# One core, an attention and a mixer: the load order of k and v, with all schedule tables redone

## The chip, the cores and the metric

One core of a Trainium2 chip. The metric is the device time of one execution in microseconds, median of several runs; lower is better. The profile is one execution taken by the hardware profiler. Engines: PE is TensorE (PEld its weight loads), DVE is VectorE, ACT is ScalarE, POOL is GpSimd, SP is SyncE, which only issues DMAs here.

## What is computed

Four batches (b = 0 to 3) of a linear attention with decay, and behind each a mixer over tokens and channels. All inputs and the output are float32.

```
B, H, S, D = 4, 8, 768, 48
for t in range(S):
    cur = einsum('bhd,bhe->bhde', u * k[t], v[t])
    y[t] = einsum('bhd,bhde->bhe', r[t], state + cur)
    state = w * state + einsum('bhd,bhe->bhde', k[t], v[t])
x = y as (B, S, 384)
h = relu(x^T @ w_tok1) @ w_tok2         # tokens: 768 -> 256 -> 768
u = x + h^T
out = u + relu(u @ w_ch1) @ w_ch2       # channels: 384 -> 1536 -> 384
```

## The kernel before, in words

**Attention.** A batch's 768 steps are six chunks of 128 (c = 0 to 5). Below, k2.3 is the load of k for batch 2, chunk 3, and so on. A load of k, v or r of one chunk is 192 KB in rows of 192 bytes (tiles kt, vt, rt, six, six and five buffers); for batches 0 and 1, r comes in windows of two chunks (tile win, 384 KB, r0.0, r0.2, r0.4). For each chunk k and r are multiplied by tables of decay (tile kr), turned, multiplied with each other to scores (at_ps), masked (AT), and multiplied with v (vb, its bfloat16 copy) to y_ps, to which the state's part is added. A state (kv_ps, S) goes from chunk to chunk. The own term (u times k times r, then times v) is summed over each head (adg) and multiplied with vb (tile ydb or yd); that last product is called own2.3 here. In batches 0 and 1 the turning is done on TensorE (tk, tr_all, result evacuated to rka and rkb), the own sum as a product (pr) and matmuls (sm); in batches 2 and 3 by DMA transposes from SP's queue (T2.3; tile rk) and with products on GpSimd (ku, rku, and two for kr: about four per chunk and own). x_b is a chunk's result. The scores of batches 2 and 3 are formed for two chunks at once (sc2.0 means chunks 0 and 1 of batch 2).

**Mixer.** Per batch: hidden (h1), back projections with the sum u (hT_ps, hx_ps; turned into uT on TensorE, or by DMA, U2.0), 24 up projections (z_ps, relu to zr) and 18 groups of down projections of 4 matmuls (h_ps), sums to osb and stores (st2.3). Weights come as seven DMAs from GpSimd's queue with conversion to bfloat16: w0 and w1 (the two token matrices, tile wtok), w2 and w3 (first third and rest of the first channel matrix), w4, w5, w6 (thirds of the second; all four kinds in tile wch). An up projection of the first four of twelve column blocks needs w2, the others w3; a down part j needs w4 + j.

**Order.** Nothing decides at run time. Some 900 tasks are added in a fixed numbering (a `Plan`); `ORDER` lists the task numbers in the order in which they are emitted, and every engine and every DMA queue works through its own tasks in that order. `BUFS` gives the buffer that each use of a tile takes, `ENGINES` picks one of the two engines for tasks that can run on either. SP's queue holds all loads, DMA transposes and nearly all stores; a load waits there until its buffer is free, and all behind it wait with it. Two tables tie the queues together:

```python
def load_weights(i):
    def f():
        t, src, how = parts[i]
        sent[i] = pool.dma_start(t, src.rearrange(how, p=128))
        if W_DEP[i] is not None:
            after(sent[i], asked[W_DEP[i]])
```

`W_DEP[i] = (b, c, what)` lets weight i be asked for only when that load has landed (what: 0 is k, 1 is r, 2 is v). `GATES[(b, c, what)] = i` does the reverse for a load and a weight. `NWARM` is the number of matmuls on zeros that only keep TensorE's clock up (kv_ps<-warm), `FILL` adds such a matmul in front of a task. All operations pass through one helper, line 281, so the profile's lines are told apart by tiles.

Of the kernel before, what the change touches and what calls it, by code (L numbers as in the profile page):

```python
# [67 lines left out]
    0, 1, 2, 0, 1, 0, 2, 1, 0, 2, 1, 0, 2, 1, 0, 1, 2, 0, 1, 2, 0, 1, 2, 0,  # L68
],
    'AT1': [  # L70
    0, 1, 2, 0, 1, 0, 2, 1, 0, 2, 1, 0, 2, 0, 1, 2, 0, 1, 2, 0, 1, 2, 0, 1,
# [11 lines left out]
    0, 1, 2, 3, 4, 1, 0, 2, 3, 4, 1, 0, 2, 3, 1, 4, 0, 2, 3, 4, 1, 0, 2, 3,  # L83
# [6 lines left out]
    0, 1, 2, 3, 4, 5, 0, 1, 4, 2, 3, 0, 4, 5, 1, 2, 3, 0, 5, 4, 1, 2, 3, 0, 5, 2, 1, 0, 3, 4,  # L90
# [3 lines left out]
    0, 1, 2, 3, 4, 5, 0, 1, 2, 3, 4, 5, 0, 1, 2, 3, 4, 5, 0, 1, 2, 3, 5, 4,  # L94
],
    'ku': [
    0, 1, 2, 0, 0, 0, 2, 0, 1, 2, 1, 2,
# [13 lines left out]
],  # L111
    'osb': [
    0, 1, 2, 0, 1, 2, 2, 2, 1, 0, 0, 1, 2, 0, 1, 2, 0, 1, 2, 0, 1, 2, 0, 1, 2,
],
    'pr': [
    0, 1, 1, 0, 1, 0, 1, 0, 1, 0, 1, 1,
# [6 lines left out]
    0, 1, 2, 0, 1, 2, 0, 1, 2, 0, 1, 2,  # L123
# [9 lines left out]
    0, 1, 2, 3, 4, 0, 1, 2, 4, 0, 3, 1,  # L133
# [9 lines left out]
    0, 1, 2, 3, 4, 0, 1, 3, 2, 4, 0, 1, 2, 3, 0, 3, 4, 1, 3, 1, 2, 0, 4, 3,  # L143
# [3 lines left out]
    0, 1, 2, 3, 4, 5, 0, 1, 3, 2, 4, 5, 0, 1, 3, 2, 4, 5, 0, 1, 3, 2, 4, 5,  # L147
],
    'win': [
    0, 1, 2, 1, 0, 2,  # L150
],
    'yd': [
    0, 1, 2, 0, 1, 2, 0, 1, 2, 0, 1, 0, 2, 1, 0, 1, 2, 0,
],
    'ydb': [
    0, 1, 0, 1, 0, 1,
],
    'zr': [
    0, 1, 2, 1, 0, 1, 2, 0,
],  # L160
}
ENGINES = [
# [9 lines left out]
]  # L172
W_DEP = [(0, 2, 2), (0, 5, 0), (0, 5, 0), (0, 3, 2), (1, 2, 2), (1, 1, 2), (1, 5, 0)]
GATES = {(2, 0, 2): 1, (2, 4, 1): 3, (3, 1, 0): 2, (3, 1, 1): 6, (3, 5, 2): 5}
NWARM = 12
WIDE_AT = [
    0, 1, 2, 3, 4, 5, 6, 7, 8, 9, 10, 11,
]
FILL = {159: 1}
POOL_ONLY = [  # L180
    2, 3,
]
# [1027 lines left out]
```

## Time and profile before

| | |
|---|---|
| median of 3 runs | 164.02 us (163.69 to 164.03) |
| the profiled execution | 163.92 us, its span 162.2 us |
| mean granted TensorE clock | 0.989 |
| PE busy | 153.4 us, 95% |
| POOL busy | 88.8 us, 55% |
| DVE, ACT busy | 112.1 us, 68.7 us |
| HBM read, written | 20.46 MB, 4.72 MB |

Times in the profile are counted from the first instruction of the span. A line of a wait view says who waited, for whom, how long in total, how many times, and the longest; a line of the chain gives start, length and what ran; a line of a timeline gives start, length, engine, operation, tiles written and read, how many, and in brackets the idle time before it and what ended that. Four rows of the page show the whole (40 slices of 4.06 us, tenths):

```
PE   6887989599999999999999999999999999999992
POOL 7149891009088899799992987999922000000000
PEclk9996899999999999999999999999999999999999
DMA  5999999999999969999999899998792055300222
```

### The profile page before, as it was taken

How to read it: one execution, taken by the hardware profiler on the slowest of the kernel's cores; microseconds unless marked ns; L12 is line 12 of the kernel's file. 1: busy time of each engine (PE TensorE's matmuls, PEld its weight loads, DVE VectorE, ACT ScalarE, POOL GpSimd, SP SyncE). 2: the span in 40 equal slices, each digit the busy share in tenths (PEclk: the TensorE clock that was granted, in tenths of full speed). 3: DMA queues.
4: the chain of work that ended last, by engine and by line, in shares of the span. 5: the costliest groups of instructions: out<-in, count | busy, mean ns of one | idle time of the engine just before them, and what ended most of it. 6: DMA issues, size and time to landing. Idle time of an engine off the chain costs nothing.

```text
span 162.2 us, 3788 instructions
## 1 busy us (share of the span) xinstructions
PE 153.4 (95%) x1458; PEld 102.5 (63%) x1459; DVE 112.1 (69%) x237; ACT 68.7 (42%) x150; POOL 88.8 (55%) x112
## 2 busy tenths in 40 slices
PE   6887989599999999999999999999999999999992
PEld 1355667367777667676667766676576666666662
DVE  6599994675697569297969928887998257523432
ACT  3988974437942354255434431144214101355000
POOL 7149891009088899799992987999922000000000
PEclk9996899999999999999999999999999999999999
DMA  5999999999999969999999899998792055300222
GB/s 130 221 206 186 161 246 236 208 178 205 200 180 204 174 137 180 230 211 141 240 213 211 177 192 163 220 207 213 121 251 103 0 124 191 73 6 0 96 98 97
DMA packets 93061, 26.89 MB, mean 166 GB/s; under 512 B 87794, under 2 KB 92148, under 8 KB 93044
## 3 DMA queue, kind: packets, MB, share of 16 engines
q1 hardware_dynamic: 90688, 23.40, 73.7%
q0 software_dynamic: 2160, 3.15, 11.5%
q8 instruction: 11, 0.18, 0.5%
q10 hardware_dynamic: 196, 0.11, 0.2%
q14 instruction: 6, 0.05, 0.1%
HBM read 20.46 MB, written 4.72 MB: 155 GB/s over the span
## 4 chain that ended last, share of the span: by engine, by line
PE 75%; DMA 11%; POOL 5%; DVE 4%; issue 2%; ACT 1%; SPq 1%; POOLq 0%; DVEq 0%
PE h_ps L281 33%; PE z_ps L281 24%; DMA wch<-in_moe_w_ch_dram 5%; PE y_ps L281 4%; PE at_ps L281 3%; DMA win<-in_r_dram 3%; PE hT_ps L281 3%; PE kv_ps L281 2%; DMA kt<-in_k_dram 2%; PE trk L281 2%; POOL kr L281 2%; POOL ydb L281 2%; DVE kr L281 1%; PE hx_ps L281 1%; SPq L281 1%
## 5 line engine op out<-in xcount | busy, mean ns | idle before, releaser
L281 PE MATMUL z_ps<-uT,wch 128*128 128x384 bf16 x288 | 52.5, 327 | 1.8 <-DMA wch<-in_moe_w_ch_dram 1.7
L281 PE MATMUL h_ps<-wch,zr 128*128 128x384 bf16 (+1 forms) x300 | 53.9, 319 | 0.0
L281 ACT ACTIVATE zr<-z_ps 128x384 bf16<-128x384 f32 x56 | 27.1, 491 | 41.0 <-PE z_ps L281 40.7
L281 PEld LDWEIGHTS <-wch 128*128 128x128 bf16 x288 | 31.1, 114 | 14.6 <-DMA wch<-in_moe_w_ch_dram 2.2
L281 PEld LDWEIGHTS <-zr 128*128 128x128 bf16 x300 | 27.6, 98 | 15.4 <-issue 0.2
L281 DVE TENSOR_TENSOR AT<-at_ps,mask 128x512 bf16<-128x512 f32 x48 | 30.9, 684 | 3.0 <-PE at_ps L281 3.0
L281 DVE TENSOR_SCALAR zr<-z_ps 128x384 bf16<-128x384 f32 x40 | 21.3, 554 | 11.9 <-PE z_ps L281 9.2
L281 POOL TENSOR_TENSOR yd<-vb,adg 128x384 f32<-128x384 bf16 x18 | 14.8, 829 | 13.0 <-DVE adg L281 5.2
L281 POOL TENSOR_TENSOR kr<-kt,wnat 128x384 bf16<-128x384 f32 x19 | 19.3, 1018 | 2.7 <-DMA kt<-in_k_dram 2.5
L281 ACT CAST vb<-vt 128x384 bf16<-128x384 f32 x22 | 11.1, 513 | 11.5 <-DMA vt<-in_v_dram 9.7
L281 PEld LDWEIGHTS <-kr 128*128 128x128 bf16 x176 | 11.4, 100 | 6.6 <-POOL kr L281 2.0
L281 DVE TENSOR_TENSOR osb<-u_sb,h_ps 128x384 f32<-128x384 bf16 (+1 forms) x16 | 8.4, 528 | 9.9 <-PE h_ps L281 9.4
L281 POOL TENSOR_TENSOR ku<-kt,u_bc 128x384 f32<-128x384 f32 x12 | 12.1, 1009 | 0.8 <-DMA kt<-in_k_dram 0.8
L281 POOL TENSOR_TENSOR rku<-ku,rt 128x384 f32<-128x384 f32 x12 | 11.9, 1004 | 0.4 <-DMA rt<-in_r_dram 0.3
L281 POOL TENSOR_TENSOR kr<-rt,wp 128x384 bf16<-128x384 f32 x12 | 12.0, 1000 | 0.0
L281 PEld LDWEIGHTS <-wtok 128*128 128x128 bf16 x78 | 7.4, 98 | 4.5
L281 DVE TENSOR_TENSOR x_b<-y_ps,yd 128x384 bf16<-128x384 f32 x18 | 9.6, 552 | 0.5 <-PE y_ps L281 0.5
L281 PE MATMUL y_ps<-vb,AT 128*128 128x48 bf16 x192 | 9.0, 184 | 0.0
L281 POOL TENSOR_TENSOR pr<-rka,rkb 128x512 bf16<-128x512 bf16 x2 | 2.3, 1152 | 11.9 <-DVE rka L281 11.9
L281 PE MATMUL h_ps<-x_b,wtok 128*128 128x384 bf16 x48 | 8.8, 326 | 0.0
L281 ACT CAST S<-kv_ps 48x192 bf16<-48x192 f32 x18 | 5.6, 311 | 6.4 <-PE kv_ps L281 3.3
L281 DVE TENSOR_TENSOR u_sb<-x_b,hT_ps 128x384 bf16<-128x384 bf16 x15 | 7.6, 548 | 0.6 <-PE hT_ps L281 0.6
(92 smaller groups left out, 183.1 us busy)
## 6 DMA issues: line engine op xcount, KB each, us to landing
kt<-in_k_dram SPq DMA_DIRECT2D x24, 192.0 KB, 5.1
vt<-in_v_dram SPq DMA_DIRECT2D x24, 192.0 KB, 4.7
out_dram<-osb SPq DMA_DIRECT2D x23, 192.0 KB, 1.9
win<-in_r_dram SPq DMA_DIRECT2D x6, 384.0 KB, 5.1
rt<-in_r_dram SPq DMA_DIRECT2D x12, 192.0 KB, 3.4
wch<-in_moe_w_ch_dram POOLq DMA_DIRECT2D x4, 384.0 KB, 6.8
wtok<-in_moe_w_tok_dram POOLq DMA_DIRECT2D x2, 384.0 KB, 5.9
wch<-in_moe_w_ch_dram POOLq DMA_DIRECT2D x1, 768.0 KB, 12.2
```

Source lines behind the costliest of these rows:

```text
L281: return lambda *args, **kw: tc.keep_in_program_order(f(*args, **kw))
```

## The change

Only tables change; no function does. Loads of k and v are listed by turns where that is possible, and `ORDER`, `BUFS`, `ENGINES`, `W_DEP`, `GATES`, `NWARM` and `FILL` are all new with it. The diff, cut (ORDER, BUFS and ENGINES hold numbers only):

```diff
 ORDER = [
-    0, 3, 22, 54, 18, 6, 16, 8, 895, 42, 59, 21, 896, 43, 39, 23, 53, 7, 13, 24, 19, 9, 2, 14, 56, 1, 11,
...
+    0, 3, 11, 54, 22, 6, 1, 895, 8, 56, 15, 42, 4, 2, 896, 12, 23, 5, 59, 20, 43, 39, 7, 24, 21, 9, 18, 46,
...
     'kt': [
-    0, 1, 2, 3, 4, 5, 0, 1, 2, 3, 4, 5, 0, 1, 2, 3, 4, 5, 0, 1, 2, 3, 5, 4,
+    0, 1, 2, 3, 4, 5, 0, 1, 2, 3, 4, 5, 0, 1, 2, 3, 4, 5, 0, 1, 2, 3, 4, 5,
...
     'vt': [
-    0, 1, 2, 3, 4, 5, 0, 1, 3, 2, 4, 5, 0, 1, 3, 2, 4, 5, 0, 1, 3, 2, 4, 5,
+    0, 1, 2, 3, 4, 5, 0, 1, 2, 3, 4, 5, 0, 1, 2, 3, 4, 5, 0, 1, 2, 3, 4, 5,
...
-W_DEP = [(0, 2, 2), (0, 5, 0), (0, 5, 0), (0, 3, 2), (1, 2, 2), (1, 1, 2), (1, 5, 0)]
-GATES = {(2, 0, 2): 1, (2, 4, 1): 3, (3, 1, 0): 2, (3, 1, 1): 6, (3, 5, 2): 5}
-NWARM = 12
+W_DEP = [(0, 3, 2), (0, 3, 2), (0, 4, 2), (0, 5, 2), (1, 0, 2), (1, 1, 2), (1, 2, 1)]
+GATES = {(1, 5, 0): 4, (2, 3, 0): 1}
+NWARM = 11
...
-FILL = {159: 1}
+FILL = {196: 1}
+TOKQ = []
```

(`TOKQ` is read nowhere.) The tables decoded, SP's queue with places counted from 0:

```
before, 0 to 34:   r0.0 r0.2 k0.0 k0.1 r0.4 v0.1 k0.3 k0.2 k0.4 v0.0 v0.2 v0.3 v0.4 k0.5 v0.5
                   r1.0 k1.0 v1.0 r1.2 k1.2 v1.1 v1.2 k1.1 r1.4 k1.3 k1.5 v1.3 k1.4 k2.0 v1.4 k2.4 r2.0 v2.0 v2.2 v1.5
after, 0 to 35:    r0.0 k0.1 r0.2 k0.2 k0.0 r0.4 v0.0 k0.3 v0.2 k0.4 v0.1 v0.3 k0.5 v0.4 v0.5
                   r1.0 k1.0 r1.2 v1.0 k1.1 v1.1 k1.2 v1.2 k1.3 r1.4 v1.3 k1.4 k1.5 k2.0 v2.2 k2.4 st0.4 v1.4 st0.5 r2.0 v1.5
before, 60 to 91:  k3.0 v3.1 r3.0 k3.3 st0.3 r3.1 k3.1 v3.0 v3.2 r3.2 T3.0 st0.1 k3.2 T3.1 U2.0 k3.4 U2.1 r3.3 k3.5 T3.2
                   r3.4 st1.3 T3.3 r3.5 st1.4 v3.3 T3.4 v3.4 st1.2 T3.5 v3.5 st1.0
after, 47 to 91:   k3.0 v2.5 T2.1 U1.1 st0.1 r2.4 k3.1 T2.3 T2.2 st0.3 v2.3 st0.0 T2.5 T2.4 v2.4 k3.2 v3.2 k3.5 r3.1 v3.0
                   r3.0 v3.1 st0.2 k3.3 T3.1 r3.5 T3.0 st1.0 v3.4 U2.1 T3.5 k3.4 r3.4 r3.2 U2.0 r3.3 v3.5 st1.3 T3.2 st1.2
                   T3.3 st1.1 v3.3 T3.4 st1.4
```

GpSimd's queue from its first product to w6 (kr0.4 is the product of k with its table, win1.1 one of r's window, wGm a table; own as above):

```
before: win0.2 kr0.3 kr0.2 kr0.4 wGm wGm w0 own0.0 own0.2 kr0.5 w1 own0.3 own0.4 w2 w3 pr1.0 win1.1 win1.1 w5 w4
        own1.0 own1.2 win1.2 kr1.3 own1.1 kr1.5 w6
after:  win0.2 kr0.3 wGm kr0.4 own0.0 own0.1 w0 kr0.5 own0.2 pr0.3 own0.4 w1 own0.3 w2 own0.5 w3 wGm pr1.0 w6 w4
        kr1.1 win1.1 own1.0 w5
```

In TensorE's queue the first of the scores of chunks 4 and 5 of batch 3 (sc3.4) is task 254 before and 249 after, the hidden layer of batch 3 task 263 and 261.

More of the change, by code (lines that the diff above doesn't have):

```diff
@@ L67 @@
     'AT0': [
-    0, 1, 2, 0, 1, 0, 2, 1, 0, 2, 1, 0, 2, 1, 0, 1, 2, 0, 1, 2, 0, 1, 2, 0,
+    0, 1, 2, 1, 0, 2, 1, 0, 2, 1, 0, 2, 1, 0, 2, 0, 1, 0, 2, 1, 0, 2, 1, 0,
 ],
     'AT1': [
-    0, 1, 2, 0, 1, 0, 2, 1, 0, 2, 1, 0, 2, 0, 1, 2, 0, 1, 2, 0, 1, 2, 0, 1,
+    0, 1, 2, 1, 0, 2, 1, 0, 2, 1, 0, 2, 1, 0, 2, 1, 0, 2, 1, 0, 2, 1, 0, 2,
 ],
@@ L82 @@
     'adg': [
-    0, 1, 2, 3, 4, 1, 0, 2, 3, 4, 1, 0, 2, 3, 1, 4, 0, 2, 3, 4, 1, 0, 2, 3,
+    0, 1, 2, 3, 4, 0, 1, 2, 3, 4, 0, 1, 2, 3, 4, 0, 1, 2, 3, 0, 4, 2, 1, 3,
 ],
@@ L89 @@
     'kp': [
-    0, 1, 2, 3, 4, 5, 0, 1, 4, 2, 3, 0, 4, 5, 1, 2, 3, 0, 5, 4, 1, 2, 3, 0, 5, 2, 1, 0, 3, 4,
+    0, 1, 2, 3, 4, 5, 1, 2, 4, 5, 0, 3, 4, 1, 2, 5, 0, 3, 4, 1, 2, 5, 3, 0, 4, 2, 5, 3, 4, 1,
 ],
@@ L93 @@
     'kt': [
-    0, 1, 2, 3, 4, 5, 0, 1, 2, 3, 4, 5, 0, 1, 2, 3, 4, 5, 0, 1, 2, 3, 5, 4,
+    0, 1, 2, 3, 4, 5, 0, 1, 2, 3, 4, 5, 0, 1, 2, 3, 4, 5, 0, 1, 2, 3, 4, 5,
 ],
     'ku': [
-    0, 1, 2, 0, 0, 0, 2, 0, 1, 2, 1, 2,
+    0, 1, 2, 0, 2, 0, 2, 1, 0, 2, 1, 1,
 ],
@@ L102 @@
     'm': [
[8 rows of a table removed]
[8 rows of a table added]
 ],
     'osb': [
-    0, 1, 2, 0, 1, 2, 2, 2, 1, 0, 0, 1, 2, 0, 1, 2, 0, 1, 2, 0, 1, 2, 0, 1, 2,
+    0, 1, 2, 0, 1, 0, 2, 0, 1, 2, 2, 1, 0, 1, 2, 0, 1, 2, 0, 1, 2, 0, 1, 2, 0,
 ],
     'pr': [
-    0, 1, 1, 0, 1, 0, 1, 0, 1, 0, 1, 1,
+    0, 1, 0, 1, 0, 1, 0, 1, 0, 1, 0, 1,
 ],
@@ L122 @@
     'rka': [
-    0, 1, 2, 0, 1, 2, 0, 1, 2, 0, 1, 2,
+    0, 1, 2, 0, 1, 2, 1, 0, 2, 1, 0, 2,
 ],
@@ L132 @@
     'rt': [
-    0, 1, 2, 3, 4, 0, 1, 2, 4, 0, 3, 1,
+    0, 1, 2, 3, 4, 0, 2, 3, 4, 0, 1, 3,
 ],
@@ L142 @@
     'vb': [
-    0, 1, 2, 3, 4, 0, 1, 3, 2, 4, 0, 1, 2, 3, 0, 3, 4, 1, 3, 1, 2, 0, 4, 3,
+    0, 1, 2, 3, 4, 0, 2, 1, 4, 3, 0, 2, 1, 4, 3, 2, 1, 4, 3, 0, 1, 2, 4, 0,
 ],
@@ L146 @@
     'vt': [
-    0, 1, 2, 3, 4, 5, 0, 1, 3, 2, 4, 5, 0, 1, 3, 2, 4, 5, 0, 1, 3, 2, 4, 5,
+    0, 1, 2, 3, 4, 5, 0, 1, 2, 3, 4, 5, 0, 1, 2, 3, 4, 5, 0, 1, 2, 3, 4, 5,
 ],
     'win': [
-    0, 1, 2, 1, 0, 2,
+    0, 1, 2, 0, 1, 2,
 ],
     'yd': [
-    0, 1, 2, 0, 1, 2, 0, 1, 2, 0, 1, 0, 2, 1, 0, 1, 2, 0,
+    0, 1, 2, 0, 1, 2, 0, 1, 2, 0, 1, 0, 1, 2, 0, 1, 2, 0,
 ],
@@ L158 @@
     'zr': [
-    0, 1, 2, 1, 0, 1, 2, 0,
+    0, 1, 2, 1, 0, 2, 1, 0,
 ],
@@ L162 @@
 ENGINES = [
[9 rows of a table removed]
-]
-W_DEP = [(0, 2, 2), (0, 5, 0), (0, 5, 0), (0, 3, 2), (1, 2, 2), (1, 1, 2), (1, 5, 0)]
-GATES = {(2, 0, 2): 1, (2, 4, 1): 3, (3, 1, 0): 2, (3, 1, 1): 6, (3, 5, 2): 5}
-NWARM = 12
[9 rows of a table added]
+]
+W_DEP = [(0, 3, 2), (0, 3, 2), (0, 4, 2), (0, 5, 2), (1, 0, 2), (1, 1, 2), (1, 2, 1)]
+GATES = {(1, 5, 0): 4, (2, 3, 0): 1}
+NWARM = 11
 WIDE_AT = [
-    0, 1, 2, 3, 4, 5, 6, 7, 8, 9, 10, 11,
+    0, 1, 2, 3, 4, 5, 6, 7, 8, 9, 10,
 ]
-FILL = {159: 1}
+FILL = {196: 1}
+TOKQ = []
 POOL_ONLY = [
```

118 rows, old and new, of tables (BUFS, ENGINES, ORDER) are left out of this document.

## The prediction

> **What bounds the kernel now.** I read the page's slices first (TensorE at 9 from the ninth slice on), then TensorE's waits, then the chain, then GpSimd's timeline where the chain enters it. Profiled execution: 163.92 us, span 162.2, 1.7 around it; the median of the runs is 0.10 higher. Sums are made on 163.92; 0.2% (0.33 us) is about what measurements of this kernel can tell from no change.
>
> TensorE's waits, longest first:
>
> ```profile
> PE z_ps L281 <- DMA wch<-in_moe_w_ch_dram: 1.7, 1, 1.7
> PE kv_ps L281 <- DVE warm L281: 1.3, 1, 1.3
> PE trk L281 <- POOL kr L281: 1.1, 2, 0.7
> ...
> PE at_ps L281 <- DVE zr L281: 0.3, 1, 0.3
> ```
>
> Only the last lies behind 32.15 us. From there to 159.3 TensorE goes from matmul to matmul. So the span is: when the first up projection (z_ps) starts, plus 127.1 us of queue, plus 2.9 us of last sum and store. The chain says what sets that start:
>
> ```profile
> 21.79 0.61 POOL ydb L281
> ...
> 22.59 0.77 POOL ydb L281
> 23.36 8.75 DMA wch<-in_moe_w_ch_dram
> ...
> 32.15 3.12 PE z_ps L281 x18
> ```
>
> GpSimd's place in its own queue decides when w2 (first part of wch1) is asked for; it lands 8.75 us later. The last copy into uT ends at 30.6 (ScalarE's timeline), 1.5 us earlier, so the weight comes last. GpSimd's timeline from 12 us:
>
> ```profile
> 12.08 3.13 POOL L281 TENSOR_TENSOR kr<-kt,wnat 128x384 bf16<-128x384 f32 x3 [0.81 <-DMA kt<-in_k_dram]
> 15.17 1.93 POOL L281 TENSOR_TENSOR wGm<-bm,wG 128x384 f32<-128x384 f32 x2
> 17.04 1.02 POOL L281 DMA_DIRECT2D wtok<-in_moe_w_tok_dram  x1
> 18.08 1.62 POOL L281 TENSOR_TENSOR ydb<-vb,adg 128x384 bf16<-128x384 bf16 x2
> 20.22 1.00 POOL L281 TENSOR_TENSOR kr<-kt,wnat 128x384 bf16<-128x384 f32 x1 [0.52 <-DMA kt<-in_k_dram]
> 21.16 0.61 POOL L281 DMA_DIRECT2D wtok<-in_moe_w_tok_dram  x1
> 21.79 1.62 POOL L281 TENSOR_TENSOR ydb<-vb,adg 128x384 bf16<-128x384 bf16 x2
> 23.36 1.59 POOL L281 DMA_DIRECT2D wch<-in_moe_w_ch_dram  x2
> ```
>
> w0, w1 and w2 land at 22.67, 27.40 and 32.10 (issue plus 5.63, 6.24 and 8.75): w2 lands 4.7 after w1, as w1 does after w0, so it queues behind w1 and follows w1's issue too.
>
> **The change, part by part.** *Work.* Decoding both tables, TensorE has the same tasks but for one warm matmul (all in the head); the one filler matmul only moves. Nine evacuations go from ScalarE to VectorE: 9 x 0.55 = 5 us more on an engine that is busy 112 of 162. GpSimd loses two products (1.0 each) and gains an own term (0.81) and a pr (1.15): -0.04. I take nothing for these: VectorE's 31% of free time hides them; one that stood on TensorE's path would cost 0.06 (0.55 against ScalarE's 0.49) to 0.55.
>
> *Gates and buffers.* The five dropped gates held loads for weights that had landed by 56.8, before four of the loads were asked for and, for v2.0, 23 us before: no gain. Strict turns of kt and vt change which consumer frees a buffer; SP stood up to 4.2 us at k2.0 before and TensorE didn't notice: 0, at most 1.
>
> *Loads of batch 0.* Bytes and queue are the same; a 192 KB load lands each 1.05 us (k0.2 12.99, k0.4 14.05, v0.0 15.11, v0.2 16.16), a window each 1.56. The eleventh lands at 16.16; with the same three windows among the first eleven it does so again, but now it is v0.1. The twelfth, v0.3, follows at 17.2.
>
> *Issue of w0 to w3.* In front of w0 GpSimd now has own0.0 and own0.1. own0.1 needs the cast of v0.1, 16.16 + 0.51 = 16.7; behind kr0.4 (15.2 to 16.2) and own0.0 (0.81) it runs 17.0 to 17.8, and w0's new wait for v0.3 (17.2) is over. So w0 is asked at 17.8, 0.8 later. Behind it: issue 1.02, kr0.5 1.00, own0.2 0.81, pr0.3 1.15, own0.4 0.81: w1 at 22.6, 1.4 later. Then issue 0.61 and own0.3 0.81: w2 at 24.0, 0.64 later; w3, behind own0.5, at 25.4, 1.2 later. The first z_ps is late by between 0.64 (8.75 after w2's issue) and 1.4 (4.7 behind a w1 that lands 6.24 after its own); middle 1.0. Outer bounds: a flight of 5.6 us for w2 (w0's, alone) lands it at 29.6, so that uT decides and z_ps starts near 30.6, 1.5 earlier; 1 us of waiting for sm0.3 or the cast of v0.4 makes it 2.4 late.
>
> uT doesn't take the weight's place: own0.5 ends near 25.6 on GpSimd, and from its add matmul at 25.84 to the last copy at 30.6 it took 4.8 before: uT is ready at 30.4 to 31.5. tk1.0 (0.22) and the turn of window 1.0 run under the wait.
>
> *w4 to w6.* w6 now stands ahead of w4 and waits for r1.2, which landed at 35.5 before. The first down needs w4, behind 21 ups (21 x 0.49), two scores (0.33 each) and smaller pieces (1.2): 12.2 after z_ps, at 45.4. If r1.2 lands by 37, w6 and w4 go out at 37.0 and 37.6; w5 and w4 went out at 39.6 and 40.2 and landed 6.1 and 7.5 later, so w4 lands at 45.1. Cost 0; if r1.2 comes 2 us later, 2. w5 follows own1.0 and v1.1 near 42, lands by 48 and is read 16.8 behind z_ps, at 50. k1.5 on SP now waits for w4, up to 3 us (its place was reached at 42.1); k2.0 and batch 2's loads stand behind it, but k2.0 left only at 47.55 before. Two stores of batch 0 stand ahead of v1.4, r2.0 and v1.5; their sums end near 52.5 and 55, v1.5 lands by 60 and is read at 62.7.
>
> *Batches 2 and 3.* GpSimd is nearly full from 54 to 117: 12 chunks x (4 x 1.0 + 0.83) = 58 us. Its longest waits there:
>
> ```profile
> POOL yd L281 <- DVE x_b L281: 3.1, 1, 3.1
> POOL kr L281 <- DMA kt<-in_k_dram: 1.2, 1, 1.2
> POOL ku L281 <- DMA kt<-in_k_dram: 0.8, 1, 0.8
> ```
>
> k3.0 and k3.1 go from places 60 and 66 of SP's queue to 47 and 53, so the 1.2 and the 0.8 may go, and some of the 3.1, as products of batch 3 stand by: 0 to 5 us gained on GpSimd. The last turn lands at 120.87 and its scores (sc3.4) start at 121.02. In the new order 2 downs (0.65), 2 y (0.37) and a kv (0.17) more lie behind sc3.4 and an up (0.49) less: 1.72 us. With nothing gained on GpSimd TensorE would wait there and end 1.72 later; that is not added to the 1.0 of the start, the later of the two counts. With 0.8 or more gained the start alone counts. Two of the three waits going, I take 0.1, and 0.7 as an end of the range.
>
> Sum: 163.92 + 1.0 + 0.1 = 165.0.
>
> **Rivals.** *A, the forecast:* late weights, 164.3 to 165.6. Chance 0.38.
>
> *B, a later feed decides:* w4 behind w6, or the last turn (T3.4, now at the end of SP's queue behind v3.3 and three stores of batch 1). For it: the slack of 0.15 us at 121.02, and 1.72 us less of it. Against: k3 comes earlier. If the last turn lands 0.6 after 120.87: 163.92 + 1.72 + 0.6 = 166.2; 165.6 to 168. Chance 0.24.
>
> *C, not slower:* w2 no longer queues behind w1. w2's landing gap is 4.7 us for 384 KB, while w3 with 768 KB lands 4.3 after w2; so w2's 4.7 held something else, and SP's queue moved 0.56 MB from 22.9 to 26.9. If w2, asked 1.4 instead of 2.2 us after w1, follows it in half of w3's 4.3, it lands at 22.6 + 6.2 + 2.2 = 31.0. Then z_ps starts 1.1 earlier, and with the 0.3 at 114 gone: 162.5 to 164.2, middle 163.2. It decides if w2 lands less than 3.3 us behind w1. Chance 0.32.
>
> *D, the cold clock.* The granted clock is the third number from the right:
>
> ```profile
> 12.00:16.00 4.00, 3.04 (x37) 2.01 (x35) 3.77 (x10) 3.35 (x10) 3.78 (x5) 0.71 1.37 187
> 16.00:20.00 4.00, 3.92 (x68) 2.82 (x68) 3.63 (x9) 3.82 (x10) 3.69 (x4) 0.86 1.31 163
> ```
>
> Two warm matmuls stood amid batch 0's scores, near 15 us; in the new order all stand before them. At 0.6 (the lowest digit of the page's clock row) these stretches' 3.04 x 0.71 + 3.92 x 0.86 = 5.5 us of work take 9.2 instead of 7.0. Less the 1.0 us of idle in them TensorE lags 1.2, and with it sm0.3, own0.3 and w2: 163.92 + 0.64 + 1.2 + 0.1 = 165.9. Chance 0.06. The Trainium skill, TensorE: Matmul & The Clock Gate, Part 1: The HAM clock gate, speaks for this rival: it says that the clock falls to half after an idle window of some 3.4 us and comes back only after about as much sustained work; at half, an estimate from that page, the stretch would take 11 us and the time would be near 167.7. The trace has 0.71 and 0.86 as means of 4 us, and 1.00 from 20 us on.
>
> That the change doesn't do what it says needs no price: k and v alternate at 35 of the 47 joints of the load order, at 25 before.
>
> **How the numbers follow.** Faster by over 0.2% (under 163.6) is most of C, 0.26. Within: C's upper end and a little of A, 0.08. Slower: 0.66. Likeliest A: 165.0, its own range 164.3 to 165.6. The range leaves out C's best and B's worst, a tenth at each side: 162.8 to 167.6.
>
> **What would show it.** Right: w1 asked near 22.6, w2 near 24.0, first z_ps near 33.1 after a wait for wch of 2 us or so, TensorE's later waits under 0.7 in all, the last turn landing at 119 to 121. B: a wait of TensorE for wch at the first downs, or at sc3.4. C: first z_ps before 32. D: a clock below 0.7 from 12 to 20 us. Wrong would be GpSimd's queue running otherwise than worked out here, or TensorE losing time in many small waits behind 33 us that no case names.

## The result and the profile after

The changed kernel takes 165.27 us, the median of 4 runs (165.25 to 166.86), against 163.86 of the kernel before in the same runs (162.69 to 164.03). The ratio is 1.0148, 95% interval 1.011 to 1.0186. A ratio here is not the quotient of the two medians: the medians differ by 1.41 us, the ratio of 1.0148 is 2.4 us. (Both come from few runs; a second measurement, p0_after, has 1.68 by medians and a ratio of 1.0119, which is 1.95.) The profiled execution took 165.28, its span 163.57, which is 1.35 more than before's 162.22. The helper's line is now L282.

First TensorE's waits, from the top of the view (who waited for whom, total, times, longest; the first two shown stand at 1.3 and 12.6 us):

```profile
PE kv_ps L282 <- DVE warm L282: 1.3, 1, 1.3
PE kv_ps L282 <- DVE vb L282: 0.9, 1, 0.9
...
PE z_ps L282 <- DMA wch<-in_moe_w_ch_dram: 0.5, 1, 0.5
PE hx_ps L282 <- DMA wtok<-in_moe_w_tok_dram: 0.3, 1, 0.3
```

The wait for w2 at the first up projection is only 0.5, where 2 was forecast, and a new one stands in front of it: the back projections (hx_ps) wait for w1. The chain enters the first up projection as before, by GpSimd's queue and the flight of w2:

```profile
24.14 0.08 DVE adg L282
...
24.30 0.78 POOL ydb L282
25.08 7.82 DMA wch<-in_moe_w_ch_dram
...
32.94 3.60 PE z_ps L282 x21
```

GpSimd's timeline shows why w1 and w2 were asked for at 23.32 and 25.08, later than the 22.6 and 24.0 of the forecast. Two waits in brackets, 0.82 and 0.38, stand in front of own0.4 and own0.3:

```profile
17.78 1.02 POOL L282 DMA_DIRECT2D wtok<-in_moe_w_tok_dram  x1
18.82 1.01 POOL L282 TENSOR_TENSOR kr<-kt,wnat 128x384 bf16<-128x384 f32 x1
19.78 0.83 POOL L282 TENSOR_TENSOR ydb<-vb,adg 128x384 bf16<-128x384 bf16 x1
20.57 1.15 POOL L282 TENSOR_TENSOR pr<-rka,rkb 128x512 bf16<-128x512 bf16 x1
22.55 0.83 POOL L282 TENSOR_TENSOR ydb<-vb,adg 128x384 bf16<-128x384 bf16 x1 [0.82 <-ACT adg L282]
23.32 0.60 POOL L282 DMA_DIRECT2D wtok<-in_moe_w_tok_dram  x1
24.30 0.82 POOL L282 TENSOR_TENSOR ydb<-vb,adg 128x384 bf16<-128x384 bf16 x1 [0.38 <-DVE adg L282]
25.08 0.81 POOL L282 DMA_DIRECT2D wch<-in_moe_w_ch_dram  x1
```

The marks of both profiles, in us from the start of the span:

| | before | after |
|---|---|---|
| w1 asked for, landed | 21.16, 27.40 | 23.32, 29.63 |
| w2 asked for, landed | 23.36, 32.10 | 25.08, 32.90 |
| last copy into uT ends | 30.63 | 32.80 |
| first up projection (z_ps) | 32.15 | 32.94 |
| last turn of batch 3 landed | 120.87 | 120.52 |
| sc3.4 starts | 121.02 | 120.56 |
| TensorE's last matmul ends | 159.25 | 160.56 |

So the start is 0.79 later, the stretch from there to sc3.4 is 1.25 shorter (88.87 to 87.62), and the stretch behind sc3.4 is 1.77 longer (38.23 to 40.00); together 1.31 of the 1.35. The middle stretch has 1.94 us less work (the 1.72 that now lies behind sc3.4, and the turn of k1.0, 0.22, that now runs ahead of the first z_ps) and is only 1.25 shorter, so TensorE loses 0.69 more in it. Little of that is recorded as idle time (0.42 us in the stretch, 0.34 before); the rest lies in matmuls that follow each other less closely, for instance 0.33 us more for the same four kv_ps<-S,ident.

What the end hangs on is best seen in the chain between 92 and 121 us. In the changed kernel it leaves TensorE for the last time at 93.18 and comes back at 120.28:

```profile
92.61 0.56 PE y_ps L282 x16
93.18 1.96 POOL kr L282 x2
...
103.42 0.78 SPq L282
...
104.26 3.27 DMA kt<-in_k_dram
...
113.47 0.97 POOL rku L282
114.44 0.38 SPq L282
...
115.49 4.15 DMA vt<-in_v_dram
...
119.72 0.52 ACT vb L282
...
120.28 0.33 PE kv_ps L282 x4
120.61 0.58 PE at_ps L282 x16
```

For 27 us the chain is products on GpSimd, SP's queue and two loads: k3.4, which SP asks for only at 104.26 behind U2.1 and T3.5, then GpSimd's products back to back, then v3.3, which SP asks for at 115.49 behind T3.3 and a store. Only then come kv3.3 and sc3.4. TensorE itself is busy with other work for nearly all of these 27 us and waits 0.26 at their end; the chain says what would have to come earlier for sc3.4 to come earlier. In the kernel before the same chain is off TensorE for 12 us, and it is back on it 6 us ahead of sc3.4 (at_ps at 121.08):

```profile
102.86 0.69 DVE AT L281
...
113.89 0.94 DVE zr L281 x2
...
114.88 1.14 PE z_ps L281 x6
...
121.08 0.55 PE at_ps L281 x16
```

### The profile page after: what moved, and what is told of

Its sections match the earlier page's. It is cut to its first block, busy times and chain, and to the rows that moved or that the text cites. A ratio compares the mean times of both kernels' runs of the same rounds, so it can differ in the third digit from the quotient of the medians.

```text
span 163.6 us, 3763 instructions
## 1 busy us (share of the span) xinstructions
PE 155.0 (95%) x1458; PEld 103.3 (63%) x1458; DVE 117.6 (72%) x246; ACT 64.0 (39%) x140; POOL 87.6 (54%) x112
## 4 chain that ended last, share of the span: by engine, by line
PE 63%; DMA 14%; POOL 10%; DVE 5%; ACT 2%; SPq 2%; issue 2%; ACTq 0%; POOLq 0%
PE h_ps L282 27%; PE z_ps L282 20%; DMA wch<-in_moe_w_ch_dram 5%; DMA vt<-in_v_dram 5%; PE y_ps L282 4%; POOL kr L282 4%; PE at_ps L282 3%; DMA win<-in_r_dram 3%; POOL rku L282 3%; PE kv_ps L282 3%; DMA kt<-in_k_dram 2%; DVE kr L282 2%; PE hT_ps L282 2%; POOL ku L282 2%; SPq L282 2%
## 5 line engine op out<-in xcount | busy, mean ns | idle before, releaser
L282 PE MATMUL h_ps<-wch,zr 128*128 128x384 bf16 (+1 forms) x300 | 53.6, 320 | 0.0
L282 PE MATMUL z_ps<-uT,wch 128*128 128x384 bf16 x288 | 51.7, 327 | 0.6 <-DMA wch<-in_moe_w_ch_dram 0.5
L282 PEld LDWEIGHTS <-wch 128*128 128x128 bf16 x288 | 31.6, 114 | 14.1 <-DMA wch<-in_moe_w_ch_dram 0.7
L282 ACT ACTIVATE zr<-z_ps 128x384 bf16<-128x384 f32 x51 | 24.9, 491 | 36.2 <-PE z_ps L282 36.0
L282 PEld LDWEIGHTS <-zr 128*128 128x128 bf16 x300 | 27.5, 98 | 15.1
L282 DVE TENSOR_TENSOR AT<-at_ps,mask 128x512 bf16<-128x512 f32 x48 | 30.6, 683 | 6.0 <-PE at_ps L282 6.0
L282 DVE TENSOR_SCALAR zr<-z_ps 128x384 bf16<-128x384 f32 x45 | 23.9, 555 | 10.3 <-PE z_ps L282 10.1
L282 POOL TENSOR_TENSOR yd<-vb,adg 128x384 f32<-128x384 bf16 x17 | 14.3, 853 | 16.4 <-DVE x_b L282 6.6
L282 POOL TENSOR_TENSOR kr<-kt,wnat 128x384 bf16<-128x384 f32 x18 | 18.2, 1013 | 3.2 <-DMA kt<-in_k_dram 2.1
L282 PEld LDWEIGHTS <-kr 128*128 128x128 bf16 x176 | 12.2, 104 | 7.9 <-issue 2.4
L282 ACT CAST vb<-vt 128x384 bf16<-128x384 f32 x21 | 10.6, 512 | 16.8 <-DMA vt<-in_v_dram 15.5
L282 DVE TENSOR_TENSOR osb<-u_sb,h_ps 128x384 f32<-128x384 bf16 (+1 forms) x16 | 8.4, 527 | 10.6 <-PE h_ps L282 8.3
L282 POOL TENSOR_TENSOR ku<-kt,u_bc 128x384 f32<-128x384 f32 x12 | 12.2, 1021 | 3.8 <-DMA kt<-in_k_dram 3.8
L282 POOL TENSOR_TENSOR rku<-ku,rt 128x384 f32<-128x384 f32 x12 | 12.2, 1017 | 0.1
L282 POOL TENSOR_TENSOR kr<-rt,wp 128x384 bf16<-128x384 f32 x12 | 12.2, 1018 | 0.0
L282 DVE TENSOR_TENSOR x_b<-y_ps,yd 128x384 bf16<-128x384 f32 x18 | 9.7, 550 | 1.0 <-PE y_ps L282 1.0
L282 DVE TENSOR_TENSOR u_sb<-x_b,hT_ps 128x384 bf16<-128x384 bf16 x15 | 7.7, 547 | 3.5 <-PE hT_ps L282 3.3
L282 PEld LDWEIGHTS <-wtok 128*128 128x128 bf16 x78 | 7.3, 98 | 4.5
L282 PE MATMUL y_ps<-vb,AT 128*128 128x48 bf16 x192 | 9.0, 186 | 0.0
L282 PE MATMUL h_ps<-x_b,wtok 128*128 128x384 bf16 x48 | 8.8, 326 | 0.0
L282 DVE TENSOR_REDUCE adg<-rku 128x8 f32<-128x384 f32 x12 | 6.6, 547 | 3.0 <-POOL rku L282 2.7
L282 PE MATMUL kv_ps<-vb,kr 128*128 128x96 bf16 x80 | 7.0, 213 | 1.2 <-DVE vb L282 0.9
```

Source lines behind the costliest of these rows:

```text
L282: return lambda *args, **kw: tc.keep_in_program_order(f(*args, **kw))
```

## The experiments

Each edit is a few lines behind the tables; a pair (a, b) moves task a in `ORDER` to just ahead of task b, all else stays. Ratios are against the kernel before on the same chip. The theories that the expectations name are S (the start alone sets the time), F (the feed, which is the loads, GpSimd's products and the turns of batches 2 and 3, sets it at sc3.4), M (several such bounds lie close together) and D (the cold clock). For the kernels with the changed kernel's TensorE order the table gives how much later (+) or earlier (-) the same matmul starts than in the changed kernel's profile, and behind it the time of that execution and the median of all:

```
at (us in the changed kernel)   32.94    80      95      110     120.56  140    execution, median
h1_weights                      +0.25   +0.22   +0.45   +0.44   +0.58   +0.58   165.85  164.93
h2_evac                         +0.07   +0.37   +0.29   +0.13   +0.48   +0.48   165.78  165.74
h3_clock                        -0.56   -0.02   +1.49   +1.27   +0.91   +0.91   166.22  165.76
f1_feed                         -0.89   +0.37   +0.80   +2.40   +1.96   +1.96   167.22  166.41
g1_start                        -1.15   -0.80   -0.90   -0.92   -0.40   -0.40   164.87  165.32
g2_feed                         +0.98   +0.99   +1.66   +3.17   +2.73   +2.72   168.01  167.01
g3_both                         -1.24   -1.20   -0.74   +0.05   -0.39   -0.40   164.92  166.18
p0_after                        -0.33   +0.78   +1.27   +1.84   +1.56   +1.56   166.83  165.34
p1_start_k34                    -1.28   -1.30   -1.56   -0.15   -0.59   -0.59   164.71  165.92
```

Each row is one execution, up to 1.5 us off the median of its kernel, so a row shows where that execution lost time and not where the median did. Behind sc3.4 (120.56) no row changes by more than 0.01. Whatever is won or lost is won or lost ahead of it, much of it between 33 and 60 and between 80 and 120 us.

### Start, evacuations, clock and feed, one at a time

**h1_weights**: w0 to w3 one or two products earlier on GpSimd's queue.

```diff
+for n, before in [(119, 137), (120, 173), (121, 209), (122, 225)]: ...
+W_DEP[0] = (0, 2, 2)
```

> The changed kernel with w0, w1, w2 and w3 each asked for earlier on GpSimd (w0 ahead of own0.0, w1 ahead of own0.2, w2 ahead of own0.4, w3 ahead of own0.5), w0 tied to v0.2 instead of v0.3. In both theories w0 goes out at 16.1 instead of 17.8, w1 near 20.5 instead of 23.3, w2 near 22.7 instead of 25.1, and the first z_ps starts at 32.4 to 32.5 instead of 32.94, because uT (last copy at 32.8, 0.3 of it a wait for w1) comes next. Theory S, the start decides: 0.4 to 0.5 us less than the changed kernel's 165.27, so 164.8. Theory F, the late feed decides (GpSimd, SP and the last turn, which lands at 120.52 just ahead of its scores at 120.56): TensorE comes earlier and waits for the last turn and for v3.3 instead, 165.1 to 165.3.

Measured: 164.93 against 163.4, ratio 1.0100 [1.0069, 1.0132]. w2 was asked for at 22.31 and landed at 29.46, 3.4 earlier than in the changed kernel, and yet the first z_ps of the profiled execution came at 33.2, since uT was late (its last copy ended at 33.7). The clock stood at half from 12.7 to 23.0 us there, longer than in the changed kernel's profile, which goes with it: with the same edit at full clock (g1_start, below) the last copy ended at 32.3. This execution says nothing on an early start. The ratio hints at some 0.3 to 0.8 us (1.0100 against 1.0148 and 1.0119 of the changed kernel), within the intervals; the medians, 1.53 apart, show nothing.

**h2_evac**: four of the nine evacuations (x_b of chunks 0.1, 0.2, 0.3 and 0.5) back on ScalarE.

```diff
+for i, e in [(24, 0), (35, 0), (42, 0), (60, 0)]:
+    ENGINES[i] = e
```

> The changed kernel with the four copies of x_b for chunks 1, 2, 3 and 5 of batch 0 back on ScalarE, which is idle 1.8 and 3.4 us there, while one of these copies (0.55 us) lies on the chain to w2. Theory S: own0.3 and w2 go out 0.5 earlier, x_b and uT come 0.5 earlier, first z_ps near 32.4, time 164.8. Theory F: first z_ps near 32.4 as well, time 165.1 to 165.3. If the prediction's cover for these moves was right (VectorE's free time), nothing at all moves: z_ps at 32.9.

Measured: 165.74, ratio 1.0145 [1.0113, 1.0177]. The two waits on GpSimd went, w1 was asked for at 22.47 and w2 at 23.87, and still w1 landed at 30.34 and w2 at 32.85:

```profile
PE hx_ps L287 <- DMA wtok<-in_moe_w_tok_dram: 2.4, 1, 2.4
```

TensorE stood 2.4 us at the back projections, and uT (33.51) came no earlier. The evacuations had cost GpSimd 1.2 us, but in this execution the weights did not land earlier for it.

**h3_clock**: the warm matmuls put back among batch 0's scores.

```diff
+FILL = {196: 1, 141: 5, 138: 2, 174: 3, 143: 2}
```

> The changed kernel with 12 filler matmuls among batch 0's first scores (5 ahead of kv0.0, 2 ahead of sc0.0, 3 ahead of sc0.2, 2 ahead of y0.0), to keep TensorE's clock up; the trace of the changed kernel has half clock from 13.71 to 20.54, the one before from 13.70 to 17.11. Theory D (cold clock): half clock for one window or none, TensorE 1 to 1.7 us earlier at 20, own0.4 and own0.3 no longer wait for sums (0.8 and 0.4 us), w2 out at 24.0, first z_ps at 32.0, time 164.4. Theory S without D: the weights follow GpSimd's own queue, z_ps at 32.6 to 32.9, time 165.0 to 165.3. An execution of the changed kernel with a mean clock of 1.000 took 165.25, which speaks against D.

Measured: 165.76, ratio 1.0144 [1.0103, 1.0186]. The clock did what the edit was for (the number right behind POOL's busy time in a row of the windows view; first the changed kernel, then this one):

```profile
12.00:16.00 4.00, 3.17 (x39) 2.71 (x40) 3.96 (x12) 2.38 (x7) 2.75 (x3) 0.71 1.46 187
16.00:20.00 4.00, 3.93 (x51) 2.97 (x51) 2.97 (x7) 3.81 (x10) 3.84 (x6) 0.50 1.22 154
```

```profile
12.00:16.00 4.00, 3.73 (x48) 2.48 (x46) 3.95 (x10) 2.45 (x9) 2.61 (x3) 1.00 1.46 189
16.00:20.00 4.00, 3.98 (x79) 2.99 (x77) 3.77 (x10) 3.84 (x12) 3.62 (x5) 1.00 1.00 149
```

A clock of 1.00 instead of 0.71 and 0.50 bought no time. The start came 0.56 earlier, and two waits for v (at 85 and 91 us) took it and more:

```profile
PE kv_ps L286 <- ACT vb L286: 1.6, 2, 1.1
```

**f1_feed**: k3.4, r3.4, v2.3 and v3.3 earlier on SP's queue.

```diff
+for n, before in [(113, 631), (114, 631), (94, 96), (112, 519)]: ...
```

> The changed kernel with four loads earlier on SP: k3.4 and r3.4 ahead of U2.1, v2.3 ahead of r2.4, v3.3 ahead of st1.3. In the changed kernel GpSimd stands 3.2 us for k3.4 at 104.3 to 107.5, and TensorE waits 0.4 for v3.3 at 119.7 and 0.26 for v2.3 at 84.8. Theory F: the last turn lands near 117.5 instead of 120.5, those waits go and the small ones at 104 to 106 with them; time = first z_ps (32.94) + work: 0.7 to 1.0 less, 164.3 to 164.6. Theory S: the feed is hidden but for the two waits, 164.6 to 165.3. If neither, and the new loads only displace others (DMA is busy at nine tenths until 113), 165.3 or more.

Measured: 166.41, ratio 1.0190 [1.0155, 1.0226]: no faster than the changed kernel and rather slower (the intervals overlap), which is the expectation's third case. GpSimd's wait for k3.4 fell from 3.2 to 0.3, but what stood behind the moved loads came late, and TensorE waited for that (its waits behind 33 us):

```profile
PE z_ps L288 <- DVE u_sb L288: 1.2, 1, 1.2
PE kv_ps L288 <- DVE vb L288: 1.1, 1, 1.1
PE at_ps L288 <- DMA rk<-kr: 0.6, 1, 0.6
PE hT_ps L288 <- ACT osb L288: 0.6, 1, 0.6
```

The second line is not of the edit's making. It stands at 40.7 us, ahead of all moved loads, behind a product of VectorE (kr<-win) that took 2.51 us instead of the 0.74 of the changed kernel's profile; p0_after, without any edit, has the same wait.

### Start and feed together, and the work behind sc3.4

**g1_start**: h1_weights and h3_clock together.

```diff
+for n, before in [(119, 137), (120, 173), (121, 209), (122, 225)]: ...
+W_DEP[0] = (0, 2, 2)
+FILL = {196: 1, 141: 5, 138: 2, 174: 3, 143: 2}
```

> The changed kernel with w0 to w3 asked for earlier on GpSimd's queue and the warm matmuls put back among batch 0's scores (both edits of the two earlier kernels together). First z_ps expected at 31.3 to 32 (changed kernel: 32.94). Theory S, the start alone counts: the time falls by as much as the first z_ps comes earlier, to 163.7 to 164.2, with no new wait behind it. Theory F, the last turn alone counts: T3.4 lands at 120.5 to 121.3 as before and the time stays at 165.0 to 165.8. Theory M, several bounds lie within 1 us of each other (start, v2.3 and v2.4 near 85 and 91 us, last turn): the time stays within 0.5 of 165.3, and TensorE's waits for vb at 85 and 91 us take what the start gives.

Measured: 165.32 over 12 runs against 163.63, ratio 1.0101 [1.0071, 1.0130]. The first z_ps came at 31.79, 1.15 earlier than in the changed kernel, with w2 landing at 31.45; the median time is the changed kernel's (165.27). In the profiled execution 0.40 of the 1.15 is left at sc3.4, and the chain shows where 0.54 of it went: a row of products on GpSimd, then T3.3.

```profile
107.57 1.00 POOL kr L290
...
112.48 4.82 DMA rk<-kr
...
117.35 0.23 PE at_ps L290
```

Theory S falls. The time is the one that M gave, though its waits at 85 and 91 us did not come, and it lies in F's range too, though the last turn (119.53) was no bound here.

**g2_feed**: the feed moved ahead at the places where SP stood waiting.

```diff
+for n, before in [(94, 573), (97, 573), (113, 631), (114, 631), (111, 624), (112, 624), (773, 750), (774, 509)]: ...
```

> The changed kernel with the feed of batches 2 and 3 moved ahead where SP stood waiting: v2.3 and v2.4 ahead of T2.3, k3.4 and r3.4 ahead of U2.1, r3.3 and v3.3 ahead of U2.0, T3.4 ahead of st1.1, and on GpSimd the product of r3.4 one place ahead of two others. T3.4 expected to land near 117 (changed kernel: 120.52), GpSimd's wait of 3.2 for k3.4 gone. S: no change, 165.2 (first z_ps at 32.9). F: sc3.4 no longer has to wait, the time falls by 0.5 to 1.7, to 163.5 to 164.7. M: TensorE has nothing to wait for but cannot come earlier than its start allows: 164.9 to 165.2.

Measured: 167.01, ratio 1.0200 [1.0151, 1.0249]. T3.4 landed at 119.91 at a sc3.4 of 123.29, so the last turn was 3.4 us early and no bound at all, and the time was the worst of all, no theory's number:

```profile
PE z_ps L288 <- DMA uT<-u_sb: 1.8, 1, 1.8
PE at_ps L288 <- DMA rk<-kr: 0.9, 1, 0.9
```

A transpose T2.x (read at 85 us) and U2.1 (read at 108 us), both behind moved loads, came late instead.

**g3_both**: g1_start and g2_feed together.

```diff
+for n, before in [(119, 137), (120, 173), (121, 209), (122, 225), (94, 573), (97, 573), (113, 631), (114, 631), ...
+W_DEP[0] = (0, 2, 2)
+FILL = {196: 1, 141: 5, 138: 2, 174: 3, 143: 2}
```

> Both edits together. S: as the early start alone, 163.7 to 164.2. F: as the early feed alone, 163.5 to 164.7. M: only here does the time fall by as much as the first z_ps comes earlier, 1.0 to 1.6 below the changed kernel: 163.6 to 164.2, while each edit alone gives less than 0.5.

Measured: 166.18, ratio 1.0153 [1.0109, 1.0197]. No theory's number. The start was 1.24 earlier, T3.4 landed at 117.92, 2.3 us ahead of sc3.4, and TensorE had lost the whole lead by 110 us, 1.05 of it to U2.1. Since each theory expected 164.7 or less, the run does not choose between S, F and M. That the feed has more places than the ones moved is a reading of the trace; no run shows a feed that is early at all of them.

**b1_behind**: the kernel before, two down projections moved from ahead of sc3.4 to just behind it.

```diff
+for n, before in [(686, 691), (687, 691), (688, 668), (689, 700)]: ...
```

> The kernel BEFORE with two down projections (2 x 0.65 = 1.30 us of TensorE work) moved from ahead of sc3.4 to just behind it, with their sum and store; nothing else. F and M: the last turn lands near 120.9 as before, TensorE waits there for about 1.1 (1.30 less the slack of 0.15), and the time rises by 1.0 to 1.3, to 164.6 to 165.2 against 163.4 to 163.9 of the kernel before. S: TensorE's work and start are the same, no change within 0.3.

Measured: 165.05 against 163.63, ratio 1.0076 [1.0041, 1.0112], which is 1.24 us (0.67 to 1.83) for 1.30 us of moved work. In the profile the start is 0.74 earlier (z_ps at 31.41), but that lead is gone by 57 us, where TensorE waits 0.61 for w6 (landed at 56.83). Just ahead of the moved work TensorE is 0.36 ahead of the kernel before, and from 125 us to the end (160.07) it is 0.82 behind: 1.18 for 1.30. Of the 1.30 that it no longer has to do ahead of sc3.4, 0.69 went into waits for VectorE there, as the chain has it:

```profile
118.58 0.60 DVE AT L287
119.17 0.48 DVE S L287
...
119.78 0.33 PE kv_ps L287 x4
120.11 0.89 PE at_ps L287 x16
```

Another 0.34 went into sc3.4 itself (the last line: 0.89, where the kernel before has 0.55), half of which ran only when the last turn had landed, at 120.37. So in the kernel before, too, work taken from ahead of sc3.4 is mostly turned into waiting there. S, which gave no change, is refuted; F and M hold in the time, but the last turn alone, F's place, has only a third of the waiting.

### The changed kernel again, one clean move, and the start of the kernel before

**p0_after**: the changed kernel, unchanged.

> The changed kernel itself, as a yardstick on the same chip as the three others. All theories: 165.0 to 165.6, 1.2 to 1.7 above the kernel before.

Measured: 165.34 against 163.66, ratio 1.0119 [1.0072, 1.0166]. Its profiled execution, the slowest of six, took 166.83 where the first took 165.28: the same program, the start 0.33 earlier, TensorE's end 1.56 later. The clock was 1.00 all through. The waits from 25 us on differ:

```profile
PE hx_ps L282 <- DMA wtok<-in_moe_w_tok_dram: 1.7, 1, 1.7
PE kv_ps L282 <- DVE vb L282: 1.0, 1, 1.0
PE at_ps L282 <- DMA rk<-kr: 0.6, 1, 0.6
PE kv_ps L282 <- ACT vb L282: 0.6, 1, 0.6
```

Behind 33 us these are waits at four places (41, 86, 99 and 104 us, the one at 99 of 0.24 for h1r), 2.4 us in all, and none of them at sc3.4. The first, 0.98 at 41 us, stands behind VectorE's product kr<-win, which took 2.39 us here; two products of GpSimd run beside it. What held it was not tried.

**p1_start_k34**: the early start of g1_start, and of the feed only k3.4 and r3.4 ahead of U2.1, where SP waited for u_sb anyway.

```diff
+for n, before in [(119, 137), (120, 173), (121, 209), (122, 225), (113, 631), (114, 631)]: ...
+W_DEP[0] = (0, 2, 2)
+FILL = {196: 1, 141: 5, 138: 2, 174: 3, 143: 2}
```

> The changed kernel with the early start of g1_start, and k3.4 and r3.4 ahead of U2.1 on SP's queue (where SP waited for u_sb anyway); nothing else of the feed moves. First z_ps near 31.8, GpSimd's wait for k3.4 (2.9 in g1_start) gone, T3.2 1 to 2 us earlier. Theory M (a feed takes what the early start gives, in the waits at 101 and 117 us that g1_start shows): these waits go and the time falls to 164.0 to 164.6, 0.7 to 1.2 below the changed kernel on the same chip. Rival N: each such move only pushes the lateness to the next transfer of SP's queue (U2.1, T3.5, U2.0): the time stays at 165.0 to 165.6.

Measured: 165.92, ratio 1.0138 [1.0086, 1.0190], above the numbers of both. The trace, of the fastest of six executions (164.71), shows the mechanism of rival N: the waits at 101 and 117 us are gone, T3.4 landed at 118.16, GpSimd waited 0.2 for k, and TensorE lost 1.31 at 105.08 to the transpose next in SP's queue:

```profile
98.21 2.60 PE h_ps L290 x16
100.81 0.17 PE at_ps L290
100.98 4.06 DMA uT<-u_sb
...
105.08 0.68 PE z_ps L290 x3
```

In it the two loads of 192 KB ahead of U2.1 cost more than the 0.21 and 0.54 of the two waits that they removed. Where the slower executions lost their time isn't known.

**b2_late**: the kernel before, w2 held until k1.0 has landed.

```diff
+W_DEP[2] = (1, 0, 0)
```

> The kernel BEFORE with w2 asked for only when k1.0 has landed (25.8 instead of 23.4 on GpSimd's queue; w3 behind it); nothing else. First z_ps expected 0.9 to 1.5 later than the 32.15 of before. The term of the forecast (start plus a fixed queue): the time rises by the same 0.9 to 1.5, to 164.5 to 165.1 where before is at 163.6. Rival: the end hangs on the feed, which does not move: less than 0.4.

Measured: 164.34 over 12 runs, ratio 1.0020 [0.9984, 1.0055]. The edit did not do what it was for: w2 was asked for at 25.48, 2.1 later than before, and landed at 31.87, 0.2 earlier; the first z_ps came at 31.92. The run tells nothing on a later start, but much on the flight of w2 (below).

**b3_late_behind**: b1_behind and b2_late together.

```diff
+for n, before in [(686, 691), (687, 691), (688, 668), (689, 700)]: ...
+W_DEP[2] = (1, 0, 0)
```

> The kernel BEFORE with both: the late w2 of b2_late, and the two down projections (1.30 us) moved behind sc3.4 as in b1_behind (which took 1.24 more than before). The forecast's clause that the later of the two counts: about the larger of the two alone, 1.2 to 1.6 above before. Rival, the two add, since the feed is itself paced by TensorE and comes later with it: 2.1 to 2.8 above before.

Measured: 165.53, ratio 1.0109 [1.0063, 1.0154], 1.8 us (1.0 to 2.5). Again the start was not late enough (z_ps at 32.29, 0.14 later), so the clause that the later of the two counts was not put to its test. As a second measurement of the work behind sc3.4 it agrees with b1_behind: just ahead of the moved work its profile is 1.98 later than that of the kernel before, behind it 3.20, so 1.22 for 1.30. In b2_late, where that work was not moved, the same two places are 1.11 and 1.12 later.

No kernel here beats the one before, and none pointed to one that would.

## Why the prediction was right, and where it was not

The number came true: 165.0 was forecast with 164.3 to 165.6 as its own range, 165.27 was measured. Its cause came true only in part, and the number is in part luck: the term that it rests on, 1.0 for a late start, is not what the time follows, and the term that it set aside, the work behind sc3.4, leads to nearly the same time. By steps:

**The start.** Case A, late weights, is what the first profile shows: the first z_ps 0.79 later (forecast 0.64 to 1.4, 1.0 taken). But the price put on it, start plus a fixed queue, is refuted. With the start 1.15 earlier g1_start takes 165.32, with 1.28 earlier p1_start_k34 takes 165.92. At most a part of it counts; the ratios of h1_weights and g1_start (1.010 against 1.0148 and 1.0119) leave room for 0.3 to 0.8 us, and the intervals overlap. That share stays open.

**The work behind sc3.4.** The prediction had it in the likeliest case as "that is not added to the 1.0 of the start, the later of the two counts", and as rival B. The 1.72 is 1.77 in the profile, and it is 40.0 from sc3.4 to the end in every profile of the changed order set beside it. On the kernel before such a move cost 1.24 for 1.30 by the ratio of b1_behind, and 1.18 and 1.22 in the traces of b1_behind and b3_late_behind, so 1.6 for 1.72. The changed kernel costs 1.41 and 1.68 by medians, 2.4 and 1.95 by ratios. So this work can account for all of it by medians and for two thirds or more by ratios; the rest is about what an earlier start has room for. But no run moves the 1.72 back ahead of sc3.4 in the changed kernel: there this cause is argued, from the kernel before and from the early starts that gained little, and not shown.

What failed in the prediction is the term "With 0.8 or more gained the start alone counts", gained on GpSimd. GpSimd's waits between 55 and 118 us did fall, from 6.1 to 4.6 us in all, but the last turn came 0.35 earlier only, since 3.2 of what is left is one wait, for k3.4, which the new order put behind U2.1 and T3.5:

```profile
POOL ku L282 <- DMA kt<-in_k_dram: 3.8, 2, 3.2
POOL yd L282 <- DVE adg L282: 0.8, 1, 0.8
```

So rival B's mechanism fits best, just below its range (1.72 with no later turn: 165.6), not at its 166.2. Its place was named too narrowly. It isn't the last turn alone: g2_feed and g3_both had T3.4 landed 2.3 and more us ahead of need and gained nothing. In executions with the changed kernel's order on SP's queue TensorE waited for v of batch 2 (at 85 and 91 us), T3.0 (101 to 104), T3.3 (117) and v3.3 (120), 0.1 to 1.1 us each, and not at the same places in each. That the feed as a whole binds is the reading that fits these waits; no edit of it made the kernel faster, so it isn't shown either. The prediction's own sign of being wrong, many small waits behind 33 us that no case names, is met by p0_after (2.4 us in four) and not by the first profile (0.42).

**Issue of w1 and w2.** Forecast 22.6 and 24.0, measured 23.32 and 25.08. The prediction added up GpSimd's own work and took "1 us of waiting for sm0.3" as an outer bound only; 1.2 us of waiting came. "VectorE's 31% of free time hides them", said of the nine evacuations, failed there in one place: with four of them back on ScalarE both waits were gone (h2_evac). In h2_evac it gained nothing, as w2's landing did not follow.

**uT.** "uT doesn't take the weight's place", ready at 30.4 to 31.5; it was ready at 32.80. The step that failed first is the end of own0.5 on GpSimd, forecast near 25.6 and measured at 26.75, behind the 1.2 us of waiting above: its add matmul ran at 27.00 instead of 25.84. From there to the last copy it took 5.8 instead of 4.8, with 0.44 for the turn of window 1.0, which now stands amid the back projections, and 0.30 for their wait for w1 (landed at 29.63 instead of 27.40). w1's own reader, the back projections, was left out of the prediction; in p0_after and h2_evac, where own0.5 came earlier, their wait for w1 (1.7 and 2.4) is the one that sets the first z_ps. But an early w1 alone doesn't bring uT back: in g1_start it landed at 25.96, own0.5 ended at 26.90, and the last copy at 32.30. A moved weight has to be followed to every reader, and each reader to its other sources.

**Rival C** was right in its mechanism: w2 landed 3.27 behind w1 (its condition was under 3.3), and its flight was 7.82, not 8.75. It did not come out, since w1 itself landed 2.2 later. Over the runs w2 landed 2.4 (p0_after) to 5.5 us (g1_start) behind w1, so the 4.7 that the prediction read as a queue is no fixed gap.

**Rival D** was right in its clock, wrong in its price. The clock was at half from 13.7 to 20.5 us (0.71 and 0.50 in the two stretches, about the 0.6 that the rival took), and at 20.5 us TensorE was 1.3 us behind p0_after, the same program at full clock; but p0_after and h3_clock, at full clock, then waited for weights or v and were no faster. The Trainium skill (TensorE: Matmul & The Clock Gate, Part 1: The HAM clock gate) gives windows of some 3.4 us in which the clock is half or full. The traces agree: half clock for 3.41 us in the kernel before, twice that in the changed kernel, three times in h1_weights. The estimate of 167.7 that was worked out from it priced as lost what lay beside the weights' flight.

**w4 to w6, buffers, gates.** Cost 0 forecast, and none of TensorE's waits names wch behind 33 us. r1.2 landed at 28.06, w4 at 42.80, and the first down started at 45.37 without a wait.

## What to carry to other kernels

When an order is tuned until many transfers arrive just in time, a late start and a late feed give the same time, and a forecast can be right in its number for the wrong one of the two: make the start earlier, and see whether the time follows. Work moved from ahead of a point that waits for its feed to behind it can cost nearly its full length, here 1.24 for 1.30, though no engine does more and no recorded wait of TensorE at that point is longer than 0.2 us. And one execution isn't the kernel: two profiles of the same program differed by 1.55 us, with four small waits in the slower one, so a difference of 1.35 has to be asked of medians and edits, not of one pair of traces.

## What the runs showed of the hardware

The landing of w2 hardly depended on when it was asked for in the kernel before: asked for at 23.36, 23.57 (b1_behind), 25.48 (b2_late) and 26.68 (b3_late_behind), it landed at 32.10, 31.36, 31.87 and 32.24. The flight of one and the same 384 KB was 8.7 to 5.6 us, and holding it back by 3.3 us cost 0.1. In the changed order the landing moved more with the issue: 22.71 (p1_start_k34), 24.00 (p0_after), 25.08 and 26.32 (g2_feed) landed at 30.67, 32.38, 32.90 and 33.88, but 22.31 (h1_weights) and 22.84 (g1_start) at 29.46 and 31.45, and w0 and w1 had moved in some of these too. What w2 queues behind was not tried; here a duration from issue to landing was no constant of a transfer.

The clock differed between executions of one program: mean 1.000, 0.979, 0.979 and 0.969 in the four first runs of the changed kernel, which took 165.25, 165.26, 165.28 and 166.86; in p0_after the execution of 166.83 had 1.000.
